# Two channels at once on even and odd rows in the first transform stage of a long-convolution and maxout kernel

## The chip, the core and the metric

The kernel runs on one core of a Trainium2 chip. A core has five engines with queues of their own: TensorE (PE; its weight loads are listed as PEld), VectorE (DVE), ScalarE (ACT), GpSimd (POOL) and SyncE (SP, which issues DMAs). Matmul results land in PSUM; everything else works in SBUF. PE, DVE and ACT reach PSUM, POOL does not. The metric is the device time of one execution in microseconds. Before the change it is 2269.31 us, the median of three runs (2269.03 to 2272.66).

## What is computed

```python
# x, v: (4, 12544, 128); the filter is the same for all four batches
h_filt = (np.maximum(pos_emb @ w1, 0) @ w2) * np.exp(-0.01 * pos)[:, None]
u = x * v
y = irfft(rfft(u, n=2*S, axis=1) * rfft(h_filt, n=2*S, axis=0), n=2*S, axis=1)[:, :S]
t = (x * y).reshape(4 * 12544, 128)
h = np.maximum(np.maximum(t @ moe_w1, t @ moe_w2), t @ moe_w3)     # 768 wide
out = h @ moe_w_out
```

A causal convolution of 12544 positions for each of 128 channels and four batches, then a maxout layer with three input matrices and one output matrix. All of it is in float32. The weights of the maxout arrive as float64 words and are converted on the chip; two of the three input matrices are kept as differences from the first (max(a, b, c) = a + max(max(b-a, 0), c-a)), and the first one is folded with the output matrix into `lin`.

## The kernel before

**The convolution in stages.** A sequence of 12544 is laid out as 98 rows (NB) of 128. Its transform of length 128 x 90 (N1 = 90) is done in two stages with a fixed small table each. The first stage works over the 98 rows, for each channel. The second one works over the 128 places within a row, and its tables differ for each of 45 pairs of frequencies (NK = 45). Then come the product with the filter's transform and the same two stages backwards.

**A unit** is four channels (`NU` = 32 units a batch). For batches 1 to 3 a unit goes through these steps, each a function that the plan places in a slot:

- `u_load` (SP): two DMAs of 196 KB, x and v with the places within a row reversed, 128 partitions x 4 channels x 98. The tiles come from the pools `inp` (3 buffers) and, for every fourth unit, `inq`.
- `u_mul` (DVE): the product x v, in place.
- `u_planes` (POOL): the low and high 16 bits of each number are copied to two planes of a tile `planes`, padded from 98 to 128 columns with zeros by a memset (lines 395 and 396).
- `u_dma` (SP): one transposing DMA of the planes into `turned`.
- `u_join` (ACT one half, DVE the other): the two halves of each number are put together again, in `uT`: 98 rows by 16 stacks of 64, for two units. Each tile `uT` belongs to two units, of which each writes a half.
- `u_first`, which is `u_products` and what it returns (line 418): the matmuls. For each of four channels, each half h and each part c (real, imaginary), a stack of uT (98 x 64) is the stationary operand and 90 columns of the table `f1q` move: 16 matmuls a unit, output in 64 partitions each, two column blocks. Line 440 copies the part h = 0 out of PSUM (ACT, `high`), and line 445 writes the sum and the difference with the part h = 1 to `spec` (two DVE operations of 360 elements).

Units 0 to 5 of batch 1 take a different way (`u_turn`): PE transposes them during the prologue, four transposes to a bank of PSUM, and ACT copies the bank out.

**The pairs of frequencies.** `spec` holds the result of the first stage for a whole batch: 128 partitions x 90 x 2 x 128 channels. When all 32 units are done, `q_load` takes rows of it for the frequencies of two steps g to a tile `sq`, in four DMAs of 32 partitions (SP, lines 467 to 471). `g_quarter` (PE, lines 496 and 506) does the second stage of step g and the backward one of step g - 3 in 64x64 blocks, `g_fold` (ACT, DVE) sums them, `q_swap`, `q_re`, `q_im` (ACT, DVE, POOL) multiply by the filter, `q_unfold` (two DVE operations, line 552) makes sum and difference, and `g_store` (POOL queue) writes the result to DRAM. I call the time in which units run a unit stage, the rest of a batch its pair stage.

**The maxout beside it.** All this runs beside the maxout of the previous batch, which is cut into 32 tiles of 392 positions and each tile into six slots (NF = 6). A slot is one `up` (four matmuls of 392 columns into two of three banks `hps`, a Relu on ACT at line 771, a max on DVE at line 774) and one `down` (two matmuls into `ops`). Each tile also needs `t_load` (DMAs), `t_sums` (two operations, on POOL while units run, otherwise on DVE), `t_last` (the last backward stage, PE, into a bank of the pairs `cps`) and a store. There are 192 slots a batch, and PE runs them in the order of the program text.

**The plan.** `conv_steps(b, done)` (line 609) gives each step a slot. A unit's place is `s = (u - done) * UNIT * per_pair + lead`; its load comes nine slots earlier, mul six, planes five, dma four, the join at s, the product two later. `UNIT` is 0.6 (line 702), `lead` is 1 for batches 2 and 3 and 6 for batch 1, whose units 0 to 5 are done in the prologue and at the start. The first pair of frequencies starts seven slots after the last unit's place. With these numbers `per_pair` is 2.63 slots for batches 2 and 3 (units every 1.58 slots, product of unit 31 in slot 51, first quarter in slot 56) and 2.71 for batch 1 (1.62, 48 and 53). A negative slot lies in the batch before.

The products of units 0 and 1 of batch 1 are made in the prologue (`unit`, line 1102), those of 2 to 4 by hand in the first slot of the maxout (lines 1195 to 1225).

## Time and profile before

| what | value |
|---|---|
| median of three runs | 2269.31 us |
| span of the profiled execution | 2267.5 us |
| PE busy | 2252.4 us (99%) |
| DVE, ACT, POOL busy | 1563.7, 1176.0, 876.7 us |
| first-stage matmuls, L428 into cps | 2960 instructions |
| ACT copy of the part h = 0, L440 | 93 times, 797 ns |
| DVE sum and difference into spec, L445 | 186 times, 789 ns |
| POOL copy to planes, L396 | 90 times, 847 ns |
| sq from spec | 264 DMAs of 128 KB, 6.4 us to landing |

One execution was recorded. Lines of the page give the engine, the line of the program, the operation, the tile written and the tiles read. Matmuls are pipelined, so the busy time of a group counts overlapping ones together; distances between starts tell their pace. A float32 matmul is listed as two instructions, and each has a weight load. "128*64" in a matmul is its rows (contraction) by its columns (output partitions). The chain that ended last is followed back from the last instruction, at each step to what released it. The rows of windows give, for each engine, the busy time and number of instructions in a stretch, then the granted clock, the mean busy share of the 16 DMA engines and GB/s.

### The profile page before, as it was taken

Reading aid. Unit: us, or ns where it says so; the run is one execution under the profiler, and the core shown is the slowest. Engines: PE = TensorE matmul, PEld = TensorE weight load, DVE = VectorE, ACT = ScalarE, POOL = GpSimd, SP = SyncE. Lnnn points to the kernel's source line nnn. Section 1 sums busy time; section 2 is a strip of 40 time slices with the busy share of each in tenths; the row PEclk is TensorE's granted clock in tenths of the full one; section 3 lists DMA queues with packets and bytes.
Section 4 is the critical chain, followed back from the end, with each engine's and each line's share of the span. In section 5 each row is a group of like instructions: output and inputs, shape, how many; then the busy total and the mean of one; then the engine's idle time right before and its main releaser. Section 6 shows DMA issues by size and latency. Waiting matters only on the chain.

```text
span 2267.5 us, 68405 instructions
## 1 busy us (share of the span) xinstructions
PE 2252.4 (99%) x27855; PEld 1356.9 (60%) x27855; DVE 1563.7 (69%) x2859; ACT 1176.0 (52%) x2131; POOL 876.7 (39%) x1090
## 2 busy tenths in 40 slices
PE   9999999999999999999999999999999999999998
PEld 8999866555555556655555556655555556666665
DVE  5589967678778667668888757667888754454443
ACT  3688844466666534456666534456666522222222
POOL 1145434223333234323333234323333326666666
PEclk9999999999999999999999999999999999999999
DMA  8788999889989599989999699889999732222221
GB/s 194 179 248 277 298 201 183 168 201 233 243 220 248 158 187 185 174 190 239 241 236 238 181 180 185 160 195 239 232 245 232 194 82 56 58 70 67 56 56 23
DMA packets 473324, 411.03 MB, mean 181 GB/s; under 512 B 327997, under 2 KB 374526, under 8 KB 473009
## 3 DMA queue, kind: packets, MB, share of 16 engines
q1 hardware_dynamic: 445929, 329.31, 64.4%
q0 software_dynamic: 26288, 75.62, 10.9%
q8 instruction: 219, 3.59, 0.7%
q10 hardware_dynamic: 792, 1.72, 0.3%
q14 instruction: 96, 0.79, 0.1%
HBM read 262.84 MB, written 84.67 MB: 153 GB/s over the span
## 4 chain that ended last, share of the span: by engine, by line
PE 99%; DMA 0%; issue 0%; ACT 0%; POOL 0%; DVE 0%; POOLq 0%; ACTq 0%; DVEq 0%
PE hps L156 45%; PE ops L156 20%; PE ops L834 6%; PE cps L428 5%; PE ps L156 4%; PE cps L156 4%; PE cps L496 3%; PE ps L165 3%; PE cps L506 3%; PE sps L1066 2%; PE gps L1048 2%; PE last L156 1%; PE ps L380 1%; PE ps L342 1%; DMA wt<-wt_const 0%; DMA zt<-zd 0%
## 5 line engine op out<-in xcount | busy, mean ns | idle before, releaser
L156 PE MATMUL hps<-gt,w_sb 128*64 128x392 f32 x6144 | 1146.2, 494 | 0.1
L771 ACT ACTIVATE hid<-hps 128x392 f32<-128x392 f32 x768 | 384.1, 500 | 699.6 <-PE hps L156 680.6
L156 PEld LDWEIGHTS hps<-gt,w_sb 128*64 128x64 f32 x6144 | 421.2, 137 | 430.8 <-issue 401.3
L774 DVE TENSOR_TENSOR hid<-hid,hps 128x392 f32<-128x392 f32 x768 | 428.0, 557 | 335.6 <-PE hps L156 323.0
L156 PE MATMUL ops<-hid,wo_sb 128*64 128x392 f32 x2304 | 477.1, 492 | 0.0
L548 POOL TENSOR_TENSOR cb<-cb,xs 128x512 f32<-128x512 f32 x135 | 173.9, 1288 | 474.7 <-DVE xs L545 384.1
L156 PEld LDWEIGHTS ops<-hid,wo_sb 128*64 128x64 f32 x2304 | 166.0, 137 | 213.1 <-issue 213.1
L521 DVE TENSOR_TENSOR cb<-cps,eo 128x512 f32<-128x512 f32 (+1 forms) x288 | 175.1, 649 | 76.1 <-ACT eo L518 76.1
L445 DVE TENSOR_TENSOR spec<-cps,high 128x360 f32<-128x360 f32 (+1 forms) x186 | 139.2, 789 | 104.7 <-ACT high L440 104.7
L789 POOL DMA_DIRECT2D out_dram<-ot x96 | 75.6, 788 | 335.2 <-ACT ot L787 282.3
L536 ACT ACTIVATE xs<-cb 32x512 f32<-32x512 f32 x270 | 169.6, 628 | 21.1 <-DVE cb L521 12.1
L537 ACT COPY xs<-cb 32x512 f32<-32x512 f32 x270 | 166.3, 616 | 3.2
L440 ACT COPY high<-cps 128x360 f32<-128x360 f32 x93 | 73.9, 797 | 169.7 <-PE cps L428 144.9
L552 DVE TENSOR_TENSOR xs<-cb 128x256 f32<-128x256 f32 x270 | 144.4, 580 | 7.7 <-POOL cb L548 7.7
L428 PEld LDWEIGHTS cps<-f1q,uT 98*64 98x64 f32 x2960 | 125.4, 137 | 26.2 <-issue 24.3
L428 PE MATMUL cps<-f1q,uT 98*64 98x90 f32 x2960 | 130.9, 241 | 0.0
L396 POOL COPY planes<-ut 128x784 uint16<-128x784 uint16 x90 | 76.3, 847 | 119.8 <-DVE ut L375 114.1
L529 POOL DMA_DIRECT2D zd<-cb x135 | 92.4, 685 | 63.7 <-DVE cb L521 60.7
L156 PEld LDWEIGHTS cps<-f4p,even 90*64 90x64 f32 x1552 | 87.5, 138 | 35.9 <-issue 34.6
L858 POOL DMA_DIRECT2D out_dram<-o x128 | 77.5, 610 | 51.5 <-DVE o L851 49.1
L156 PE MATMUL cps<-f4p,zt 90*64 90x49 f32 x1552 | 95.8, 222 | 0.0
L156 PE MATMUL cps<-f4p,even 90*64 90x49 f32 x1552 | 94.5, 220 | 0.0
(152 smaller groups left out, 3150.5 us busy)
## 6 DMA issues: line engine op xcount, KB each, us to landing
ht<-hd SPq DMA_DIRECT2D x264, 256.0 KB, 6.5
wt<-wq_const SPq DMA_DIRECT2D x144, 256.0 KB, 6.2
zd<-cb POOLq DMA_DIRECT2D x135, 256.0 KB, 5.7
zt<-zd SPq DMA_DIRECT2D x384, 90.0 KB, 3.0
sq<-spec SPq DMA_DIRECT2D x264, 128.0 KB, 6.4
ut<-in_xr_dram SPq DMA_DIRECT2D x128, 196.0 KB, 4.0
ut<-in_vr_dram SPq DMA_DIRECT2D x128, 196.0 KB, 4.4
xT<-in_x_dram SPq DMA_DIRECT2D x256, 98.0 KB, 3.4
```

Source lines behind the costliest of these rows:

```text
L156: nc.tensor.matmul(out[64 * h:64 * h + 64], lhsT[:, 64 * h:64 * h + 64], rhs, start=start, stop=stop, skip_group_check=True)
L428: nc.tensor.matmul(ps[64 * c:64 * c + 64, 256 * i + h * N1:256 * i + (h + 1) * N1], t[:, 2 * ((at + i) % 8) + h].rearrange("n r t -> n (r ...
L445: nc.vector.tensor_tensor(out=spec[:, :, a, at:at + n], in0=v[:, 1], in1=highs[0], op=op)
L521: nc.vector.tensor_tensor(out=cb[:, a, lo:hi], in0=ps[:, lo:hi], in1=eo[:, lo:hi], op=op)
L529: nc.gpsimd.dma_start(zd[b][2 * z:2 * z + 2].rearrange("k c t a f -> (k c t) a f"), zss.pop(z))
L536: nc.scalar.mul(xs[at:at + 32], xt[at + 32:at + 64], -1.0)
L537: nc.scalar.copy(xs[at + 32:at + 64], xt[at:at + 32])
L548: nc.gpsimd.tensor_tensor(out=xts[g], in0=xts[g], in1=xs[:], op=ALU.add)
L552: nc.vector.tensor_tensor(out=ab[:, q], in0=y[:, 0], in1=y[:, 1], op=(ALU.subtract, ALU.add)[q])
L771: nc.scalar.activation(h[:], pa[:, 0:N], Relu)
L774: nc.vector.tensor_tensor(out=h[:], in0=h[:], in1=pb[:, 0:N], op=ALU.max)
L834: nc.tensor.matmul(ps[64 * c:64 * c + 64, 0:H2], w, rhs[:, H2 * c:H2 * c + H2], start=start, stop=True, skip_group_check=True)
```

## The change

The first stage of batches 1 to 3 is split by even and odd rows. The 98 rows become two sets of 49 (HB); the even ones sit in partitions 0 to 48 of `uT`, the odd ones in 64 to 112. `u_planes` sorts the columns in this way (one memset, now two copies of half the size), so that the transposing DMA delivers both sets; `u_turn` does it with eight matmuls against the identity in place of four transposes, and two copies by ACT. The table `f1e` has 49 rows in each half and only every second of the frequencies (45 real, 45 imaginary columns), since the others follow from sums and differences of the two sets.

A call of `u_products(x)` now belongs to two units: of each it takes two channels (d picks the unit's channels, and the 64 output partitions). It is 2 x 2 x 2 x 2 = 16 matmuls of 49 x 64 by 90 columns: the row set p picks partitions 0 to 48 or 64 to 112 and one of two banks, d picks the output partitions. ACT copies the bank of the even set (`high`), DVE writes sum and difference with the bank of the odd set to a new tile `sums` (two operations of 360), and POOL makes the second level of sums from it, into `spec`: two operations of 180 elements and four of 90. Two calls serve two units and stand in the same slot, at odd units, moved by one or two slots where t_last is.

`spec` now has the units' channel halves in the partitions and the real and imaginary parts in the free dimension, so `q_load` issues eight DMAs in place of four, in pieces of 64 numbers. `u_join` has ACT copy both halves. `q_unfold` gives its second operation to POOL. `inq` goes. `UNIT` is 0.8 with a lead of -14 for batches 2 and 3 and 0.7 with a lead of 6 for batch 1: `per_pair` is 2.61 and 2.60 slots, units come every 2.09 and 1.82 slots, the last products are in slots 52 and 53, the first quarters in 57 and 58.

```diff
-    f1q = np.stack([np.concatenate([up.real, up.imag], 1), f1], 1)
+    f1e = np.zeros((64 + NB // 2, 2, N1))
+    for p in range(2):
+        for h, t in enumerate((up, a)):
+            t = t[p::2, ::2]
+            f1e[64 * p:64 * p + NB // 2, h] = np.concatenate([t.real, t.imag], 1)
...
-        return inp if u < EARLY or u % 4 < 3 else inq
+        return inp
 
     def u_load(b, u):
-        c, g0 = divmod(u, NG // 4)
+        c, g0 = divmod(u if b == 0 else u // 2 + u % 2 * (NU // 2), NG // 4)
...
-            uts[u] = uts[u + 1] = utp.tile([NB, 16, 2, 32], FP32, tag="uT", name="uT")
-        ps = state["turn"]()
-        turn(u, ps)
-        nc.scalar.copy(uts[u][:, 8 * (u % 2):8 * (u % 2) + 8],
-                       ps[0:NB, :].rearrange("n (s t r) -> n s r t", s=8, r=2))
+            uts[u] = uts[u + 1] = utp.tile([P, 16, 2, 32], FP32, tag="uT", name="uT")
+        ps, (a, _) = state["turn"](), us.pop(u)
+        for i in range(4):
+            for p in range(2):
+                nc.tensor.matmul(ps[64 * p:64 * p + HB, i * P:(i + 1) * P], a[:, i, p::2], eye[:],
+                                 start=(i == 0), stop=True, skip_group_check=True)
+        for n in (0, 64):
+            nc.scalar.copy(uts[u][n:n + HB, 8 * (u % 2):8 * (u % 2) + 8],
+                           ps[n:n + HB, :].rearrange("n (s t r) -> n s r t", s=8, r=2))
...
-        pl_ = cvp.tile([P, 2, 4, P], U16, tag="cb", name="planes", bufs=3)
-        nc.gpsimd.memset(pl_[:, :, :, NB:], 0)
-        nc.gpsimd.tensor_copy(
-            pl_[:, :, :, 0:NB], a[:].bitcast(U16).rearrange("p s (n h) -> p h s n", h=2))
+        pl_ = cvp.tile([P, 2, 4, P], U16, tag="pl", name="planes", bufs=3)
+        w = pl_[:].rearrange("p h s (e m) -> p h s e m", e=2)
+        nc.gpsimd.memset(pl_[:].rearrange("p h s (e m) -> p (h s e) m", e=2)[:, :, HB:], 0)
+        for h in range(2):
+            nc.gpsimd.tensor_copy(
+                w[:, h, :, :, 0:HB],
+                a[:].bitcast(U16).rearrange("p s (m e h) -> p h s e m", e=2, h=2)[:, h])
...
-            copies[h](
-                uts[u][:, 8 * (u % 2):8 * (u % 2) + 8].rearrange(
+            nc.scalar.copy(
...
-    def u_products(u, i0=0, n=4, ps=None, tag="eo"):
-
-
-        t = uts[u] if i0 + n < 4 else uts.pop(u)
-        held = ps is not None
-        ps = (ps if held else state["bank"]())[:, 0:256 * n]
-        at = 4 * u + i0
-        for i in range(n):
+    def u_products(x, banks=None, tag="eo"):
+
+
+        u, w = x - x % 2, x % 2
+        t = uts[u]
+        held = banks is not None
+        if not held:
+            ps = state["bank"]()
+            banks = ps[:, 0:512], ps[:, 512:1024]
+        for i in range(2):
             for h in range(2):
-                for c in range(2):
-                    nc.tensor.matmul(
-                        ps[64 * c:64 * c + 64, 256 * i + h * N1:256 * i + (h + 1) * N1],
-                        t[:, 2 * ((at + i) % 8) + h].rearrange("n r t -> n (r t)"),
-                        f1q[:, h, c * N1:(c + 1) * N1],
-                        start=(i % 2 == 0 and h == 0), stop=True, skip_group_check=True)
-        v = ps.rearrange("p (s m) -> p s m", m=256)[:, :, 0:2 * N1].rearrange(
-            "p s (h k) -> p h k s", h=2)
-        highs = []
+                for p in range(2):
+                    for d in range(2):
+                        nc.tensor.matmul(
+                            banks[p][64 * d:64 * d + 64, N1 * (2 * i + h):N1 * (2 * i + h + 1)],
+                            t[64 * p:64 * p + HB, 8 * d + 4 * w + 2 * i + h].rearrange(
+                                "n r t -> n (r t)"),
+                            f1e[64 * p:64 * p + HB, h], start=(i == 0 and h == 0), stop=True,
+                            skip_group_check=True)
+        at = 2 * x
+        v = spec[:].rearrange("p (k x) a (c d) -> p x a c k d", x=2, c=2)[..., at:at + 2]
+        made = []
 
         def top():
-            high = cvp.tile([P, n, D], FP32, tag=tag, name="high", bufs=2 if tag == "eo" else 3)
-            highs.append(high[:, :, 0:N1].rearrange("p s k -> p k s"))
-            nc.scalar.copy(highs[0], v[:, 0])
+            high = cvp.tile([P, 4 * N1], FP32, tag=tag, name="high", bufs=3 if tag == "xs" else 2)
+            nc.scalar.copy(high[:], banks[0][:, 0:4 * N1])
+            made.append(high)
 
         def both(ops=(0, 1)):
-            for a in ops:
-                op = (ALU.add, ALU.subtract)[a]
-                nc.vector.tensor_tensor(out=spec[:, :, a, at:at + n], in0=v[:, 1],
-                                        in1=highs[0], op=op)
+            if len(made) < 2:
+                made.append(cvp.tile([P, 2, 4 * N1], FP32, tag=state["wide"][0], name="sums",
+                                      bufs=state["wide"][1]))
+            high, sums = made
+            for k in ops:
+                nc.vector.tensor_tensor(out=sums[:, k], in0=high[:], in1=banks[1][:, 0:4 * N1],
+                                        op=(ALU.add, ALU.subtract)[k])
+                y = sums[:, k].rearrange("p (i h c k) -> p h c k i", i=2, h=2, c=2)
+                for a in range(2):
+                    for c in range(2) if k else (slice(None),):
+                        nc.gpsimd.tensor_tensor(
+                            out=v[:, k, a, c], in0=y[:, 1, c], in1=y[:, 0, 1 - c if k else c],
+                            op=(ALU.add, ALU.subtract)[a ^ (1 - c) if k else a])
...
-                nc.sync.dma_start(
-                    t[64 * r + 32 * c:64 * r + 32 * c + 32, 0:n].rearrange(
-                        "p x k a d -> p (x k a d)"),
-                    spec[64 * c + 32 * r:64 * c + 32 * r + 32, 2 * g:2 * g + 2 * n].rearrange(
-                        "p k a d -> p (k a d)"))
+                for d in range(2):
+                    at, of = 64 * r + 32 * c, 64 * d + 32 * r
+                    nc.sync.dma_start(
+                        t[at:at + 32, 0:n].rearrange(
+                            "p x k a (d f) -> p d (x k a) f", d=2)[:, d],
+                        spec[of:of + 32, 2 * g:2 * g + 2 * n].rearrange(
+                            "p k a (c f) -> p c (k a) f", c=2)[:, c])
...
-        nc.vector.tensor_tensor(out=ab[:, q], in0=y[:, 0], in1=y[:, 1],
-                                op=(ALU.subtract, ALU.add)[q])
+        (nc.vector, nc.gpsimd)[q].tensor_tensor(
+            out=ab[:, q], in0=y[:, 0], in1=y[:, 1], op=(ALU.subtract, ALU.add)[q])
...
-        lead, low = (1, -NT * NF) if b > 1 else (6, 0)
+        lead, low, UNIT = (-14, -NT * NF, 0.8) if b > 1 else (6, 0, 0.7)
...
-            at(int(s + 2), 1, u_first, u)
+            if u % 2:
+                on = int(s + 2)
+                on += (0, 0, 2, 1, 0, 0)[on % NF]
+                at(on, 1, u_first, u - 1)
+                at(on, 1, u_first, u)
...
-        for h in range(2):
-            u_first(u, 2 * h, 2)
+        top, both = u_products(u, (bank(), bank()), "x")
+        top()
+        both()
```

## Prediction

> **What bounds the kernel now.** I read the page first: busy times, then the chain that ended last.
>
> ```profile
> PE 2252.4 (99%) x27855; PEld 1356.9 (60%) x27855; DVE 1563.7 (69%) x2859; ACT 1176.0 (52%) x2131; POOL 876.7 (39%) x1090
> PE 99%; DMA 0%; issue 0%; ACT 0%; POOL 0%; DVE 0%; POOLq 0%; ACTq 0%; DVEq 0%
> ```
>
> PE is the bound from end to end, and its instructions run in program order: whatever shortens its stream shortens the kernel, and whatever makes it wait lengthens it one for one. So I need the pace of the stream, not the busy column (which counts overlapping matmuls together). The timeline of PE gives it as the distance between starts. A unit of the first stage, and a short 64x64 stage in the prologue:
>
> ```profile
> 903.83 1.41 PE L428 MATMUL cps<-f1q,uT 98*64 98x90 f32 x32
> 905.07 1.49 PE L156 MATMUL hps<-gt,w_sb 128*64 128x392 f32 x8
> ...
> 30.43 1.46 PE L165 MATMUL ps<-f1q,uT 98*64 98x90 f32 x32
> 31.82 1.74 PE L342 MATMUL ps<-w_sb,specH 64*41 64x64 f32 x64
> 33.48 1.08 PE L380 MATMUL ps<-eye,ut 128*98 128x128 f32 x8
> ```
>
> One unit takes 905.07 - 903.83 = 1.24 us for 32 instructions (16 fp32 matmuls, two passes each): 38.9 ns apiece. L342, in 64x64 blocks over 64 columns, takes 33.48 - 31.82 = 1.66 us for 64: 26 ns apiece. The quarter stage shows 64x64 blocks over 128 columns, and what it costs to go in and out of them:
>
> ```profile
> 1112.64 0.83 PE L156 MATMUL ops<-hid,wo_sb 128*64 128x392 f32 x4
> 1113.40 0.67 PE L496 MATMUL cps<-sq,wt 64*64 64x128 f32 x16
> 1113.89 0.62 PE L506 MATMUL cps<-xs,wt 64*64 64x128 f32 x16
> 1114.33 0.62 PE L496 MATMUL cps<-sq,wt 64*64 64x128 f32 x16
> 1114.76 0.62 PE L506 MATMUL cps<-xs,wt 64*64 64x128 f32 x16
> 1115.31 1.54 PE L156 MATMUL hps<-gt,w_sb 128*64 128x392 f32 x8
> 1116.68 0.83 PE L156 MATMUL ops<-hid,wo_sb 128*64 128x392 f32 x4
> ```
>
> The third group follows the second after 0.44 us for 16: 27.2 ns apiece. Entry and exit cost more: the "ops" group before it lasts 0.76 us (0.66 elsewhere), the first 0.49, the last 0.55, the "hps" group after it 1.37 (1.32 elsewhere): 0.10 + 0.05 + 0.11 + 0.05 = 0.31 us a visit.
>
> **PE, the gain.** After the change two units together are 32 matmuls, so still 64 instructions, over 90 columns in 64x64 blocks. No row has that shape. L342 (64 columns) says 26 ns, the quarter stage (128 columns) 27.2. If four blocks simply ran twice as fast as today's two, 38.9 / 2 = 19.5 ns. I take 26, since going from 128 columns to 64 hardly moved the pace, which looks like a floor per instruction. Two units: 64 x 0.026 + 0.31 = 1.97 us, against 2.48 now: 0.51 saved, 48 pairs in batches 1 to 3: 24.5 us. By 27.2 ns it is 20.7, by 19.5 it is 44. Back goes the turning of units 0 to 5 of batch 1: four transposes at 0.126 us (the eight after 33.48 take 1.01) become eight two-pass matmuls, 16 instructions at about 0.06 (half of 0.126, one pass of 64 columns' width): 0.5 more for each of six, 3 us. Net 21.5 us, bounds 18 to 41.
>
> **ACT and DVE.** Each unit's second join copy moves from DVE (0.58) to ACT (0.78), and units 0 to 5 get a second 0.6 us eviction. The sums stay two DVE operations of 360, but contiguous. Half of q_unfold (135 x 0.58) leaves DVE. ACT is busy 23 of 50 us in a unit stage and DVE 35, so these lie beside PE and I cost them at nothing; without that cover the 90 join copies would be 70 us.
>
> **POOL, the new work.** The rows nearest in kind, and the share of POOL in a unit stage (850 to 900) and in a pair stage (1100 to 1150):
>
> ```profile
> L548 POOL TENSOR_TENSOR cb<-cb,xs 128x512 f32<-128x512 f32 x135 | 173.9, 1288 | 474.7 <-DVE xs L545 384.1 <-ACT hid L771 67.5 <-ACT eo L518 8.4
> L396 POOL COPY planes<-ut 128x784 uint16<-128x784 uint16 x90 | 76.3, 847 | 119.8 <-DVE ut L375 114.1 <-DMA ut<-in_vr_dram 4.0 <-DMA turned<-planes 1.8
> L804 POOL TENSOR_TENSOR hid<-hid 128x392 f32<-128x392 f32 x48 | 47.4, 1016 | 0.0
> L977 POOL COPY spec<-wo_sb 128x256 f32<-128x256 f32 x3 | 1.7, 596 | 2.5 <-PE ps L165 2.5
> 850.00:900.00 50.00, 50.00 (x654) 30.97 (x652) 35.44 (x62) 22.82 (x40) 22.01 (x32) 1.00 0.94 185
> 1100.00:1150.00 50.00, 50.00 (x592) 26.57 (x594) 40.90 (x71) 31.36 (x57) 15.74 (x17) 1.00 1.00 245
> ```
>
> A call of u_products adds six two-input operations, 720 elements in all (two of 180, four of 90). L548 and L804 (medians 1.27 and 1.02 us) give 2.1 ns an element and 0.2 us a start: 720 x 2.1 + 6 x 0.2 = 2.7 us. But those rows are contiguous, and the new operations read every element 720 bytes from the last and write runs of two. The nearest row with short runs is L977: 0.53 us (median) for 256 in runs of four, where L396's 1.07 ns an element gives 0.27, so about 1 ns an element extra. One such extra makes 3.4 us a call; on both inputs and the output, 4.9. I take 2.9, near the rows of the same operation, and keep 1.5 (no start cost) to 4.9. The planes become a memset (0.30) and two copies, 1.05 together.
>
> Now the room. A tile of the unit stage is six slots of up and down (1.98 each), 0.66 for lin, 0.92 for t_last: 13.5 us, plus units. In batches 2 and 3 units come every 0.8 x 2.61 = 2.09 slots, 2.87 a tile at 0.99 us: 16.3 us of PE. POOL: the two sums of t_sums 2.6, an output issue 0.8, 2.87 x (2.9 + 1.35) = 12.2: 15.6, so 96%. In batch 1 (0.7 x 2.60 = 1.82 slots, 3.3 units a tile) PE needs 16.8 and POOL 3.4 + 14.0 = 17.4: over by 0.6 for 7.6 tiles, 5 us, of which the head start of planes (issued five slots, some 13 us, before the join) hides most. I charge 3 us, bounds 0 to 100. Behind a late sum on POOL stand the planes, behind them the transposing DMA on SP and every load SP has after it, then ACT's join, then PE.
>
> The Trainium skill speaks against this change here: "GPSIMD Engine Reference", section 7, says that a read whose step exceeds 8 bytes costs about 2.9 cycles an element where a near one costs 1.9. No row here shows such a read. By it (an estimate: one cycle at 1.2 GHz more on each of two inputs) a call would take 2.7 + 1.2 = 3.9 us, and the total would land about 30 us above before.
>
> **The loads of sq.** q_load issues eight DMAs instead of four, in 256-byte pieces instead of 4096. On SP, four take 2.42 us of the 13.5 between two quarter pairs; SP's issues fill 159 of 230 us in 1050 to 1280, and four more a pair make 69% into 87%. On the DMA engines, the packet records show 4096-byte packets of this queue at 235 ns in that window and 256-byte ones at 18 (median) to 28 (mean) in 850 to 950: 128 x 235 / 16 = 1.9 us a pair becomes 2048 x 18..28 / 16 = 2.3 to 3.6, where the share is already 0.91 to 1.00. Today the last sq lands 3 to 9 us before its quarter; four more issues eat 2.4 of that. What is late next is the quarter itself. I charge 0.1 us for each of 69 pairs, 7 us; bounds 0 (the slack holds) to 0.6 a pair, 41.
>
> The lead of -14 moves the loads of three units and their transposes into the end of the previous pair stage; u_first itself starts at slot -8, after the last q_load has read spec, so I see no new wait on spec. The pool inq goes, but units come a third less often: nothing, unless POOL is late, which is priced above.
>
> **Sum.** 2267.5 - 21.5 + 3 + 7 = 2256. The profiled span lies 1.8 us under the median of 2269.3, so 2258.
>
> **Rivals.** First, POOL becomes the bound of the unit stages. The strided reads and the 96% speak for it, the unshaken 1.27 us of its contiguous sums against. It decides from about 3.0 us a call; at 3.4, POOL needs 17.0 a tile in batches 2 and 3 (0.7 over, 11 tiles each) and 19.1 in batch 1 (2.3 over): 15 + 17 = 32, less 10 that the head start absorbs: 2267.5 - 21.5 + 22 + 7 + 1.8 = 2277, slower. Second, the sq loads: at 0.6 us a pair, 2269.3 - 21.5 + 3 + 41 = 2292. The DMA share of 1.00 speaks for it, the slack of 3 to 9 us against. Third, no floor at 26 ns: 2269.3 - 41 + 10 = 2238; the quarter stage's 27.2 at full columns speaks for it, L342 against. Fourth, the blocks do not pair by rows and nothing is gained on PE: 2282; the 64x64 rows all but exclude it.
>
> **Chances.** My forecast (2245 to 2264) 0.52, POOL 0.22, sq 0.16, no floor 0.07, no pairing 0.03. What a measurement can tell from no change is 0.2%, 4.5 us: faster than 2264.8 takes my forecast, the third rival and the mild end of the first, 0.57; the same 0.09; slower 0.34. The range is 2238 to 2294: below it some 5%, above it the hard ends of the first two, some 12%.
>
> **What would show it.** Right: L428's successor at 1.6 to 1.8 us for 64 instructions, POOL's six operations summing to under 3.0 us a call, planes copies without a growing distance from the unit's product, quarter starts still 13.5 us apart. Wrong: POOL busy 50 of 50 in a unit stage, "hid" or "high" of ACT waiting on "turned", DVE's sums waiting for POOL, or PE in L496 waiting on "sq<-spec".

## The result, and the profile after

The changed kernel takes 2381.57 us, the median of five runs (2377.82 to 2397.18), beside 2270.2 us of the kernel before on the same chip: a ratio of 1.050 (1.0478 to 1.0522). It is 111 us slower, where 2258 was forecast with a range up to 2294. The profiled execution is the slowest of the five; its span is 2395.3 us, 127.8 us over the span of before.

The page, busy times and chain, as they were shown of the kernel before:

```profile
PE 2272.1 (95%) x27927; PEld 1316.7 (55%) x27927; DVE 1569.8 (66%) x2624; ACT 1215.6 (51%) x2223; POOL 1338.5 (56%) x1893
PE 36%; DMA 8%; SPq 3%; DVE 3%; POOL 2%; issue 1%; ACT 0%; DVEq 0%; POOLq 0%; ACTq 0%
```

The shares of the chain are of the whole span. After the change the chain can be followed back only to 1122 us, so its shares add up to 53%, of which PE has 36: PE is no longer alone in it, as it was with 99% before. The stretches that the prediction used (columns: PE, PEld, DVE, ACT, POOL busy, granted clock, DMA share, GB/s) show where:

```profile
850.00:900.00 50.00, 45.66 (x552) 22.82 (x550) 33.53 (x44) 22.45 (x42) 45.61 (x77) 0.93 0.74 132
1100.00:1150.00 50.00, 50.00 (x552) 25.71 (x546) 36.92 (x64) 32.10 (x58) 21.25 (x24) 1.00 1.02 230
```

In a unit stage PE idles 4.3 of 50 us, at a granted clock of 0.93 where it was 1.00, and POOL is busy 45.6 where it was 22.0, without its DMA issues. To see what each stage lost, I take from the traces the distance between the starts of the same maxout tile's first product with `lin`, tile by tile. Against the kernel before, the start up to the first of these tiles is 5.3 us longer, the unit stages (tiles 0 to 9 of each batch, and 27 to 31 of the batch before, where the next units lead in) 72 us, the pair stages (tiles 10 to 26, and the end of the last batch) 50 us.

**PE's own part did get shorter, more than forecast.** The timeline, start and length of a group:

```profile
920.60 1.48 PE L446 MATMUL cps<-f1e,uT 49*64 49x90 f32 x64
922.01 1.54 PE L164 MATMUL hps<-gt,w_sb 128*64 128x392 f32 x8
```

Two units take 922.01 - 920.60 = 1.41 us, 22 ns an instruction, where they took 2.48. A group of 32 of the same instructions (at 285.00 us) takes 0.78, so the second 32 cost 0.63, 19.7 ns apiece, and the way in and out costs some 0.15. As the forecast said of such blocks, the neighbours grow too: the four-instruction group before takes 0.75 us in place of 0.66, the eight-instruction one behind 1.37 in place of 1.32. That leaves 2.48 - 1.41 - 0.15 = 0.92 us a pair of units, 44 us over 48 pairs. So the losses are not 127.8 but about 172 us, most of them in the unit stages.

108 of the 172 are waits: PE idles 2395.3 - 2272.1 = 123 us of the span, before 15. Some 38 more are a slower clock: its mean over the span is 0.980, before 0.999, and by the trace's record of it PE does 77 us of its work at half clock. 16 of the 20 stretches at half clock begin during a wait of PE of 1.6 us or more, or within 1.5 us after it. What remains, some 26 us, isn't placed.

**POOL's new work, by groups** (busy, mean ns of one, then idle before):

```profile
L472 POOL TENSOR_TENSOR spec<-sums 128x90 f32<-128x90 f32 x384 | 187.9, 522 | 0.0
L472 POOL TENSOR_TENSOR spec<-sums 128x180 f32<-128x180 f32 x192 | 154.2, 825 | 57.2 <-DVE sums L467 56.9
L410 POOL COPY planes<-ut 128x392 uint16<-128x392 uint16 x180 | 97.5, 577 | 31.1 <-DVE ut L383 31.1
...
L383 DVE TENSOR_TENSOR ut<-ut 128x392 f32<-128x392 f32 x128 | 209.2, 1635 | 38.5 <-DMA ut<-in_vr_dram 36.0 <-PE ps L388 1.3 <-PE ps L173 0.7
```

The last one in the kernel before:

```profile
L375 DVE TENSOR_TENSOR ut<-ut 128x392 f32<-128x392 f32 x128 | 75.9, 595 | 20.3 <-DMA ut<-in_vr_dram 20.2
```

A call costs 2 x 0.825 + 4 x 0.522 = 3.74 us. The surprise is u_mul on DVE, which nothing changed: its mean is 1635 ns in place of 595. One of the places, in the timeline:

```profile
901.10 6.65 POOL L472 TENSOR_TENSOR spec<-sums 128x180 f32<-128x180 f32 x12
901.13 8.27 DVE L383 TENSOR_TENSOR ut<-ut 128x392 f32<-128x392 f32 x1
907.72 1.25 POOL L774 TENSOR_TENSOR even<-zt 90x512 f32<-90x512 f32 x1
909.05 1.48 POOL L774 TENSOR_TENSOR zt<-zt 90x512 f32<-90x512 f32 x1
909.32 1.02 DVE L808 TENSOR_TENSOR hid<-hid,hps 128x392 f32<-128x392 f32 x2
909.92 2.88 PE L164 MATMUL hps<-gt,w_sb 128*64 128x392 f32 x8 [6.47 <-DVE hid L808]
```

u_mul begins as POOL's twelve sums do and ends 8.27 us later, after POOL has got through them and the first of t_sums without a pause. It ends soon after the 0.08 us between the two sums of L774. The max of the maxout stands behind it on DVE, and PE waits 6.47 us for that max. The wait costs more than its length: the eight matmuls behind it take 2.88 us where such a group takes 1.54 (at 922.01 above), and the granted clock is recorded at half there, from 905.8 to 916.0 us. Of the 96 u_muls of batches 1 to 3, 35 last over 1 us; the 96 together are 138 us over 0.555 us each. Not every u_mul that meets POOL's sums is held like this one: of the 44 that begin while a sum runs, 24 are through in less than 1 us, and 15 take 3 to 8.3 us. What decides between them was not found.

PE's longest waits over the whole span (total us, times, longest):

```profile
PE hps L164 <- DVE hid L808: 54.4, 19, 8.2
PE cps L526 <- DMA sq<-spec: 16.7, 23, 2.1
PE cps L164 <- POOL zt L774: 9.6, 10, 1.0
```

The first is the wait for the max behind DVE. The second is the sign of the pair stages: PE, in the quarter's product L526, now waits for `sq`; before it never did. The third and a smaller one of the same kind, 12.0 us together, are for the sums of t_sums on POOL (L774), which come late to t_last; two more, 7.2 us, are for those that DVE makes, so that t_sums costs 19.2 us in all. The units' product L446 waited 0.3 us in all, and never for its input `uT`.

### The profile page after: what moved, and what is told of

It is laid out like the page before. It is cut to its first block, busy times and chain, and to the rows that moved or that the text cites. A ratio compares the mean times of both kernels' runs of the same rounds, so it can differ in the third digit from the quotient of the medians.

```text
span 2395.3 us, 69820 instructions
## 1 busy us (share of the span) xinstructions
PE 2272.1 (95%) x27927; PEld 1316.7 (55%) x27927; DVE 1569.8 (66%) x2624; ACT 1215.6 (51%) x2223; POOL 1338.5 (56%) x1893
## 4 chain that ended last, share of the span: by engine, by line
PE 36%; DMA 8%; SPq 3%; DVE 3%; POOL 2%; issue 1%; ACT 0%; DVEq 0%; POOLq 0%; ACTq 0%
PE hps L164 20%; PE ops L868 5%; PE ops L164 5%; DMA sq<-spec 3%; DMA ht<-hd 2%; DMA wt<-wq_const 1%; POOL spec L472 1%; PE cps L164 1%; DMA zt<-zd 1%; PE last L164 1%; DMA xT<-in_x_dram 1%; PE cps L536 1%; PE cps L526 1%; SPq L497 1%; DVE hid L808 1%
## 5 line engine op out<-in xcount | busy, mean ns | idle before, releaser
L164 PE MATMUL hps<-gt,w_sb 128*64 128x392 f32 x6144 | 1170.5, 503 | 55.9 <-DVE hid L808 54.4
L808 DVE TENSOR_TENSOR hid<-hid,hps 128x392 f32<-128x392 f32 x768 | 427.1, 557 | 422.4 <-PE hps L164 405.9
L164 PE MATMUL ops<-hid,wo_sb 128*64 128x392 f32 x2304 | 485.2, 500 | 0.0
L472 POOL TENSOR_TENSOR spec<-sums 128x90 f32<-128x90 f32 (+1 forms) x576 | 335.9, 623 | 57.2 <-DVE sums L467 56.9
L383 DVE TENSOR_TENSOR ut<-ut 128x392 f32<-128x392 f32 x128 | 209.2, 1635 | 38.5 <-DMA ut<-in_vr_dram 36.0
L426 ACT COPY uT<-turned 113x512 uint16<-113x512 uint16 x180 | 125.9, 770 | 4.3 <-DMA turned<-planes 4.2
L526 PE MATMUL cps<-sq,wt 64*64 64x128 f32 x2160 | 96.7, 280 | 25.0 <-DMA sq<-spec 16.7
L467 DVE TENSOR_TENSOR sums<-high,cps 128x360 f32<-128x360 f32 x186 | 85.9, 522 | 49.2 <-ACT high L458 49.2
L582 DVE TENSOR_TENSOR xs<-cb 128x256 f32<-128x256 f32 x135 | 94.3, 712 | 34.2 <-POOL cb L578 34.2
L410 POOL COPY planes<-ut 128x392 uint16<-128x392 uint16 x180 | 97.5, 577 | 31.1 <-DVE ut L383 31.1
L582 POOL TENSOR_TENSOR xs<-cb 128x256 f32<-128x256 f32 x135 | 113.8, 861 | 1.1
```

Of the source, the lines that this page charges most:

```text
L164: nc.tensor.matmul(out[64 * h:64 * h + 64], lhsT[:, 64 * h:64 * h + 64], rhs, start=start, stop=stop, skip_group_check=True)
L383: nc.vector.tensor_tensor(out=a[:], in0=a[:], in1=v[:], op=ALU.mult)
L426: nc.scalar.copy(uts[u][0:HR, 8 * (u % 2):8 * (u % 2) + 8].rearrange("n s r t -> n (s r t)").bitcast(U16).rearrange("n (s r t h) -> n h s ...
L472: nc.gpsimd.tensor_tensor(out=v[:, k, a, c], in0=y[:, 1, c], in1=y[:, 0, 1 - c if k else c], op=(ALU.add, ALU.subtract)[a ^ (1 - c) if k e ...
L526: nc.tensor.matmul(ps[64 * a:64 * a + 64, at:at + D], w[64 * r:64 * r + 64, k, a, :], t[64 * r:64 * r + 64, k, a, :], start=(k == 0), stop ...
L582: (nc.vector, nc.gpsimd)[q].tensor_tensor(out=ab[:, q], in0=y[:, 0], in1=y[:, 1], op=(ALU.subtract, ALU.add)[q])
```

## The experiments

All are medians of the device time; the kernel before ran beside each of them at 2270.1 to 2271.5 us. Stage columns are us of the profiled span against the kernel before, taken as above. What follows the last of the counted tiles stands in no column; it is 2.6 to 3.4 us longer in split_pool and in the runs from all3 on, all3_act aside, and within 0.6 us of before in the others.

| run | us | ratio | start | unit stages | pair stages |
|---|---|---|---|---|---|
| the change | 2381.6 | 1.050 (1.0478 to 1.0522) | +5 | +72 | +50 |
| sums_dve | 2357.5 | 1.038 (1.0364 to 1.0399) | +8 | +30 | +48 |
| unfold_dve | 2411.4 | 1.062 (1.0571 to 1.066) | +7 | +77 | +61 |
| sums_split | 2405.0 | 1.059 (1.0573 to 1.0611) | +6 | +77 | +50 |
| before_burst | 2270.5 | 1.000 (0.999 to 1.0009) | 0 | 0 | 0 |
| before_burst2 | 2279.1 | 1.0035 (1.0022 to 1.0048) | 0 | +10 | 0 |
| before_sq8 | 2314.7 | 1.019 (1.0167 to 1.0219) | +2 | +1 | +45 |
| before_sq8big | 2299.8 | 1.012 (1.0097 to 1.0146) | +3 | +2 | +28 |
| before_sq4fine | 2277.5 | 1.0037 (1.002 to 1.0054) | +4 | 0 | +10 |
| sq_pool | 2342.7 | 1.032 (1.0302 to 1.0333) | +7 | +27 | +35 |
| sq_big | 2345.4 | 1.033 (1.0297 to 1.0354) | +7 | +30 | +35 |
| sums_apart | 2320.3 | 1.023 (1.0205 to 1.0247) | +5 | -12 | +54 |
| all3 | 2292.9 | 1.010 (1.0086 to 1.012) | +8 | -13 | +25 |
| all3_unfold | 2287.5 | 1.007 (1.0054 to 1.0089) | +7 | -11 | +23 |
| all3_act | 2403.7 | 1.058 (1.0537 to 1.0618) | +6 | -3 | +130 |
| all3_close | 2329.4 | 1.026 (1.0241 to 1.0282) | +5 | +29 | +23 |
| sq_early | 2270.5 | 1.000 (0.9989 to 1.0008) | +8 | -14 | +5 |
| sq_early_split | 2258.5 | 0.994 (0.9929 to 0.9958) | +8 | -25 | +5 |
| split_pool | 2322.3 | 1.023 (1.021 to 1.0249) | +7 | +37 | +5 |

### Who holds DVE

**sums_dve**: the change with its second-level sums on DVE.

```diff
-                        nc.gpsimd.tensor_tensor(
+                        nc.vector.tensor_tensor(
                             out=v[:, k, a, c], in0=y[:, 1, c], in1=y[:, 0, 1 - c if k else c],
```

> The changed kernel with the second level of sums on DVE instead of POOL, all else as changed. Theory A (POOL's unbroken run of 12 two-input operations, 7.5 us a pair, keeps DVE from starting u_mul, which reads two SBUF tiles: 8.27 us in the trace, with the max behind it and PE idle 7.15 us): u_mul falls back to about 0.6 us, the unit stages lose their 72 us of excess and keep PE's gain; DVE pays some 1.2 us a call. 2381 - 72 - up to 48 + 0 to 50 of DVE bursts, so 2265 to 2330, the pair stages' excess of 49 us unchanged. Theory B (the unit stages lose because POOL is simply too slow for its share, 3.74 us a call): about the same time, but then u_mul would have been long only where POOL's queue was full. Theory C (the loss lies in the wider spacing or in joins on ACT): no change, 2370 to 2385.

2357.5 us, above the 2330 that theory A allowed. The mean of u_mul is back at 0.589 us, the mean granted clock rises from 0.980 to 0.993, and the unit stages lose 30 us in place of 72, though DVE now does all the sums. What is left is seen in the same place of the timeline:

```profile
905.54 0.75 DVE L472 TENSOR_TENSOR spec<-sums 128x90 f32<-128x90 f32 x4
906.20 0.56 DVE L808 TENSOR_TENSOR hid<-hid,hps 128x392 f32<-128x392 f32 x1
906.67 0.56 DVE L383 TENSOR_TENSOR ut<-ut 128x392 f32<-128x392 f32 x1
906.81 0.88 PE L164 MATMUL hps<-gt,w_sb 128*64 128x392 f32 x4 [1.79 <-DVE hid L808]
```

The sixteen sums of two calls run on DVE from 900.91 to 906.20, and the max behind them makes PE wait 1.79 us.

**before_burst and before_burst2**: the kernel before with a POOL load that nobody needs, twelve sums of the change's shapes after every fourth unit, from a weight table to a scratch tile. In the first run each sum overwrites the last one's place, so that some of them start 0.08 us after the one before has ended; in the second each has its own place and they follow without a pause.

```diff
     def u_first(*args):
         u_products(*args)()
+        if len(args) == 1 and args[0] > 5 and args[0] % 4 == 3:
+            burst(args[0] % 8 == 3)
```

> The kernel before, plus 12 POOL additions after every fourth unit (two of 180 and four of 90 elements, twice, from the resident output weights to a scratch tile that nothing reads; alternately with the change's distant reads and with near ones). POOL stays under its capacity: 7.5 us for four units of 1.2 us planes each. Theory A: u_mul and other DVE operations with two SBUF inputs stretch to as much as a burst, PE idles behind the max: 2270 + 20 to 90. Theory B: nothing waits for the scratch tile and POOL keeps up: 2268 to 2275. The near bursts against the distant ones give the price of a distant read: 0.39 against 0.52 us for 90 elements if it costs one cycle an input, equal if it costs nothing.

> The burst of 12 POOL additions on the kernel before once more, now each to a place of its own, so that no addition waits for the last one. The first burst had a gap of 0.08 us between any two, and u_mul started within it. Theory A, sharpened (DVE's two-input operations get in only when POOL leaves a gap): u_mul of up to 7 us where it meets a burst, and 2275 to 2310. If bursts without gaps hold nothing up either: 2268 to 2273, and theory A falls.

2270.5 and 2279.1 us. The same u_mul meets the same burst in both. With the pauses:

```profile
871.05 1.81 DVE L375 TENSOR_TENSOR ut<-ut 128x392 f32<-128x392 f32 x1
871.62 8.24 POOL L465 TENSOR_TENSOR idle<-wo_sb 128x180 f32<-128x180 f32 x12
```

and without:

```profile
871.35 7.68 DVE L375 TENSOR_TENSOR ut<-ut 128x392 f32<-128x392 f32 x1
871.91 6.69 POOL L465 TENSOR_TENSOR idle<-wo_sb 128x180 f32<-128x180 f32 x12
```

With pauses u_mul is through after 1.81 us, while POOL's second sum runs, which takes 1.01 us in place of 0.82; without them it is held to the end of the run, 7.68 us, and that tile of the maxout is 6.8 us longer. So the holding is shown by itself, in a kernel that has nothing else of the change, and it can last over the whole run of POOL's operations. It doesn't always: of the 12 u_muls that overlap one of the 21 bursts without pauses, one more is held, for 2.67 us, and ten are through in less than 0.8 us. That the total is only 9 us comes from there. What these bursts hold more often is DVE's half of u_join, a uint16 copy with a single input in SBUF: its mean is 924 ns where the kernel before has 585, its longest 5.03 us where that has 1.47. The change has this copy on ACT.

The Trainium skill names a cause: "SBUF — State Buffer", section "SBUF: two separate sides", says that DVE and GpSimd share a pair of ports under an exclusive lock, which a DVE operation with both inputs in SBUF needs against a GpSimd operation that reads SBUF, and that whoever comes first has it "for the whole instruction". u_mul has both inputs in SBUF; the max L808 takes one from PSUM and keeps its 557 ns. The runs agree on who blocks whom, and for the u_muls that are through after one sum on how long; but others stay out over 6.7 us of twelve instructions, not one. No run here shows the ports themselves.

**sums_split**: of the six sums of a call the two of 180 elements stay on POOL, the four of 90 go to DVE.

```diff
-                        nc.gpsimd.tensor_tensor(
+                        (nc.gpsimd, nc.vector)[k].tensor_tensor(
```

> The changed kernel with the sums' half on POOL (the two operations of 180) and the half of the differences (four of 90) on DVE. By theory A the runs of POOL are 1.65 us long and wait for DVE in between, u_mul stays under 2.5 us; DVE's burst per pair is 3.6 us instead of 5.1 in the run with all sums on DVE, which cost PE a wait of 1.8 us at the max: 2335 to 2355, against 2357.5 there. By theory B (POOL's load): POOL needs 12.2 us a tile of 16.3, the same. If DVE's length were not what keeps PE waiting, 2355 to 2370.

2405.0 us, the slowest but one, far above every expectation. u_mul is nearly free here, as theory A said (a mean of 0.659 us), and the unit stages lose 77 us all the same. The groups of DVE's sums, here and in sums_dve:

```profile
L472 DVE TENSOR_TENSOR spec<-sums 128x90 f32<-128x90 f32 x384 | 186.0, 543 | 3.3
```

```profile
L472 DVE TENSOR_TENSOR spec<-sums 128x90 f32<-128x90 f32 x384 | 77.7, 265 | 3.3
```

The same operation takes twice as long when POOL works on the other half at the same time, 108 us more in all; these sums too have both inputs in SBUF. Here the holding falls on DVE's own sums in place of u_mul. Sharing these sums between the two engines was worse than giving all of them to either.

**split_pool** asks the same of the best arrangement found (sq_early_split, below): everything as there, only the second-level sums go back to POOL.

```diff
-                        nc.vector.tensor_tensor(
+                        nc.gpsimd.tensor_tensor(
                             out=v[:, k, a, c], in0=y[:, 1, c], in1=y[:, 0, 1 - c if k else c],
```

> Base: the run sq_early_split (2258.5 us), everything else as there. Edit: the second-level sums go back to GpSimd, as the change has them; a call is still cut in two, so POOL gets two sums of 180 elements or four of 90 at a time. Theory (POOL's run of sums holds a DVE operation with two inputs in SBUF until the run ends): u_mul is held for some 2 us where the runs meet it and the sums reach spec later, 2265 to 2300 us. Rival (it was only the length of the burst; in short runs POOL relieves DVE): 2245 to 2258 us.

2322.3 us, 64 more than with DVE, outside of what either side expected. Its stretch of a unit stage:

```profile
850.00:900.00 50.00, 46.59 (x608) 23.16 (x608) 36.87 (x46) 22.17 (x42) 47.09 (x82) 0.97 0.80 154
```

POOL is busy 47.1 of 50 us, and its output stores (0.79 us each, about three in 50 us) nearly fill the rest. And u_mul is held all the same, 117 us over its usual length: with next to no pause on POOL, short runs of sums join up into long ones. How much of the 64 us each of the two takes can't be told from this run.

### The loads of sq

**before_sq8, before_sq8big, before_sq4fine**: the kernel before with its four sq loads per pair cut in eight of 256-byte pieces, in eight of 2 KB pieces, and kept at four with 256-byte pieces (a tile with a gap of two numbers after every 64). The destinations of the loads, in this order:

```diff
-                    t[64 * r + 32 * c:64 * r + 32 * c + 32, 0:n].rearrange(
-                        "p x k a d -> p (x k a d)"),
+                for d in range(2):
...
+                        "p x k a (d f) -> p d (x k a) f", d=2)[:, d],
...
+                for k in range(2):
...
+                            "p x k a d -> p (x k) (a d)")[:, at:at + n],
...
+                        "p x k a d f -> p (x k a d) f")[:, :, 0:64],
```

> The kernel before, with each load of sq as two DMAs in pieces of 64 numbers (256 bytes), as the change has it. Theory E: PE waits on sq in the pair stages, 2270 + 45 = 2315. Theory D: the slack of 3 to 9 us hides it, 2270 to 2278.

> The kernel before, with each load of sq as two DMAs of half the rows each: eight issues a pair as in the change, but pieces of 2 KB. If the 44 us of the run with fine pieces come from SP's issuing (8 x 0.73 us a pair and more), 2300 to 2315; if from the number of packets, 2270 to 2278.

> The kernel before, with the four DMAs of sq kept, but in pieces of 256 bytes (the tile sq is padded after every 64 numbers, so that nothing runs on). If packets cost: 2300 to 2315. If issues cost: 2270 to 2280.

2314.7, 2299.8 and 2277.5 us: 44, 29 and 7 more than before. The number of loads is most of it, the short pieces a smaller part. SP's queue in before_sq8 and in the kernel before, a pair's loads:

```profile
1105.29 8.34 SPq L468 DMA_DIRECT2D sq<-spec  x8
```

```profile
1085.65 3.45 SPq L467 DMA_DIRECT2D sq<-spec  x4
```

Eight loads keep SP 8.34 us where four kept it 3.45 (the medians over all pairs are 7.7 and 3.0), and PE's wait for sq in L497 goes from nothing to 20.0 us. The 44 us are nearly what the pair stages of the change lose (50).

**unfold_dve**: the change with both halves of q_unfold on DVE, to see whether POOL's half was the pair stages' loss.

```diff
-        (nc.vector, nc.gpsimd)[q].tensor_tensor(
+        (nc.vector, nc.vector)[q].tensor_tensor(
```

> The changed kernel with both operations of q_unfold on DVE again. Theory D (the pair stages lose 49 us because q_unfold on POOL comes late or holds DVE's two-input operations back): the pair stages return to the time before, 2381 - 45 = 2336. Theory E (they lose it to the 8 fine-grained loads of sq a pair of steps): 2375 to 2385, PE still waits on sq.

2411.4 us, 30 slower, above both theories: it isn't. DVE is fuller in the pair stages and they lose 61.

**sq_pool and sq_big**, on the kernel of sums_dve: half of the eight loads on POOL's queue; or all eight on SP in 2 KB pieces, with spec laid out so that the pieces are long.

```diff
-                    nc.sync.dma_start(
+                    (nc.sync, nc.gpsimd)[d].dma_start(
...
-        v = spec[:].rearrange("p (k x) a (c d) -> p x a c k d", x=2, c=2)[..., at:at + 2]
+        v = spec[:].rearrange("p g a m -> p (g a m)").rearrange(
+            "p (c k x a d) -> p x a c k d", c=2, x=2, a=2, d=64)[..., at:at + 2]
...
-                        t[at:at + 32, 0:n].rearrange(
-                            "p x k a (d f) -> p d (x k a) f", d=2)[:, d],
+                        t[at:at + 32, d, 0:n].rearrange("p x k a f -> p (x k a f)"),
```

> Base: the changed kernel with its second-level sums on DVE (2357.5 us). Edit: of the eight sq loads of a pair, the four with d = 1 are issued on POOL's queue, the four with d = 0 stay on SP; pieces stay 256 bytes. Theory (what the pair stages lose, some 43 us of span over the three batches, is SP's time to issue eight loads where there were four): most of the loss goes, 2357 - 35 = about 2320 us, 2305 to 2338, and the gain lies in tiles 10 to 26 of each batch. Rival (the 256-byte pieces load the DMA queues, whoever issues them): within 8 us of 2357.

> Same base (2357.5 us). Edit: spec and the sq tile are laid out so that each of the eight sq loads moves pieces of 2 KB instead of 256 bytes; all eight stay on SP. Theory of SP's issues: only what the pieces themselves cost goes, by the two tests on the kernel before (44 us with small pieces, 30 with 2 KB) some 13 us, so 2344 us, 2334 to 2352. Rival (the pieces are the cost): the 43 us of the pair stages go, about 2318 us, under 2328.

2342.7 and 2345.4 us. sq_big came as SP's theory said, sq_pool gained 15 us where 35 were expected. PE's quarter products in sums_dve, then in sq_pool:

```profile
L526 PE MATMUL cps<-sq,wt 64*64 64x128 f32 x2160 | 97.4, 280 | 16.3 <-DMA sq<-spec 12.2 <-DMA wt<-wq_const 3.2 <-issue 0.2
```

```profile
L526 PE MATMUL cps<-sq,wt 64*64 64x128 f32 x2160 | 96.7, 278 | 15.5 <-issue 10.6 <-DMA sq<-spec 4.3 <-DMA wt<-wq_const 0.4
```

The named wait fell from 12.2 to 4.3 us, but L526 idles nearly as long, now under "issue", which means that the profile names no releaser. sq_early, below, shows in a later kernel that such a wait is still one for sq. Relieving SP helps in part; the wait under "issue" fits loads on POOL's queue that come late too.

### Bunching, spacing, and a version of the change that is faster

**sums_apart**, on sums_dve: the two calls of a pair in neighbouring slots.

```diff
-                on += (0, 0, 2, 1, 0, 0)[on % NF]
+                on += (0, -1, 2, 1, 0, 0)[on % NF]
                 at(on, 1, u_first, u - 1)
-                at(on, 1, u_first, u)
+                at(on + (u < NU - 1), 1, u_first, u)
```

> Same base (2357.5 us). Edit: the two calls of a pair of units are put in two neighbouring slots instead of one, so that DVE gets 8 sums in a row instead of 16. Theory (what is left of the unit stages' loss is DVE's burst of 5.1 us, behind which the next max waits and PE idles 1.8 us): the unit stages with their lead-in lose some 10 to 25 us less, 2332 to 2348 us. Rival (the loss there comes from where the units stand and how widely they are spaced, not from the burst): 2352 to 2362 us.

2320.3 us, 37 less, more than expected: the unit stages go from 30 us over the kernel before to 12 under it. **all3** adds both edits of sq to it:

> Same base with the three edits together: pieces of 2 KB, half of the sq loads on POOL's queue, the calls of a pair in neighbouring slots. If the two theories hold, the pair stages come back to their old time and the unit stages nearly so: 2357 - 40 - 17 = about 2300 us, 2275 to 2318. If something else holds either loss, over 2318 us. A time under 2270 us would mean that the gain on PE, some 48 us by the 1.0 us saved a pair, comes through as well.

2292.9 us, within its bounds. Then three single edits to all3: q_unfold on DVE alone (all3_unfold), the half of the loads on ACT's queue in place of POOL's (all3_act), and the units as close as in the kernel before (all3_close: UNIT 0.6, lead 1 and 6).

```diff
-        (nc.vector, nc.gpsimd)[q].tensor_tensor(
+        (nc.vector, nc.vector)[q].tensor_tensor(
...
-                    (nc.sync, nc.gpsimd)[d].dma_start(
+                    (nc.sync, nc.scalar)[d].dma_start(
...
-        lead, low, UNIT = (-14, -NT * NF, 0.8) if b > 1 else (6, 0, 0.7)
+        lead, low, UNIT = (1, -NT * NF, 0.6) if b > 1 else (6, 0, 0.6)
...
+                on = min(on, int(share * per_pair + lead) + 2)
```

> Base: the kernel of the run all3 (2292.9 us). Edit: both halves of q_unfold on DVE, as the kernel before had them. Theory (what is left of the pair stages' loss, some 8 us in each, is PE's second half of a quarter, L537, waiting for a half that POOL makes late, behind its products and its sq issues): the pair stages lose 4 to 8 us less each, 2270 to 2282 us. Rival (it is the sq loads, still eight a pair, that come late, and DVE gets fuller): 2290 to 2315 us.

> Same base (2292.9 us). Edit: the four sq loads with d = 1 on ACT's queue instead of POOL's. Theory of POOL's lateness: POOL is free of 2.0 us of issues a pair, ACT gets them; the pair stages gain 2 to 5 us each where ACT has room, 2278 to 2290 us. Rival (ACT, which hands PE its relu tiles, is held by the issues and their waits): 2295 to 2320 us.

> Same base (2292.9 us). Edit: the units stand as close as in the kernel before (lead 1 and 6, 0.6 of a pair's slots each), the last pair's sums held ahead of the first sq load. Theory (the wider spacing gives DVE and POOL room for a pair's sums): the unit stages lose 5 to 20 us, 2298 to 2313 us. Rival (the spacing only moves work from one tile to another): 2288 to 2297 us.

2287.5, 2403.7 and 2329.4 us. The first lies between its two theories: the wait of PE for POOL's half, 3.6 us in all3, is gone, but the quarter's first product is as late as ever. On ACT the loads are worst of all, 111 us more: they stand behind ACT's relus there, and sq makes PE wait 30.3 us; whether it is only that wasn't tried. The wider spacing, with the earlier lead, is a part of the change that helps: without it the unit stages lose 41 us more, twice the most that was expected.

**sq_early and sq_early_split**, on all3_unfold: the loads three slots earlier; then each call's sums cut in two, k = 0 in its slot and k = 1 in the next.

```diff
-                at(s - 4, 0, q_load, g, min(2, NK - g))
+                at(s - (7 if g else 4), 0, q_load, g, min(2, NK - g))
...
-                at(on, 1, u_first, u - 1)
-                at(on + (u < NU - 1), 1, u_first, u)
+                for i, v in enumerate((u - 1, u)):
+                    if u < NU - 1:
+                        at(on + i, 1, u_begin, v)
+                        at(on + i + 1, 0, u_end, v)
+                    else:
+                        at(on, 1, u_first, v)
```

> Base: the run all3_unfold (2287.5 us), in which L527, the quarter's products with sq, still takes some 5 us longer in the pair stage of a batch than before and nothing else there does. Edit: from the second pair on, the sq loads are put three slots earlier, seven ahead of their quarter instead of four; their number, pieces and queues stay. Theory (the loads are late because eight take longer to issue and land than four): the pair stages lose 4 to 7 us less each, 2268 to 2280 us. Rival (SP and the DMA queues have no time left there, so that earlier loads push others back): 2284 to 2300 us.

> As sq_early, and each call's sums are cut in two: k = 0 in its slot, k = 1 in the next, so that DVE gets four sums in a row instead of eight. Theory (PE's stalls of some 9 us in the unit stage of a batch, under ops<-hid and hps, are waits for a max behind DVE's sums): 5 to 8 us less in each batch than sq_early, together 2250 to 2266 us, under the kernel before. Rival (the stall is that of the two PSUM banks, which are now held longer): as sq_early or up to 20 us slower.

2270.5 and 2258.5 us, both as their theories said. The quarter's product in all3_unfold and in sq_early, where only the time of the loads differs:

```profile
L527 PE MATMUL cps<-sq,wt 64*64 64x128 f32 x2160 | 94.3, 277 | 10.6 <-issue 10.6
```

```profile
L527 PE MATMUL cps<-sq,wt 64*64 64x128 f32 x2160 | 85.7, 276 | 0.0
```

The wait is gone and the busy time is the 85.7 us of the kernel before. sq_early_split is faster than it, by 0.57% (0.42 to 0.71). The busy times of its page, and the stretch of a unit stage:

```profile
PE 2227.3 (99%) x27927; PEld 1298.6 (58%) x27927; DVE 1629.3 (72%) x3335; ACT 1216.8 (54%) x2223; POOL 1044.1 (46%) x1458
```

```profile
850.00:900.00 50.00, 50.00 (x622) 25.06 (x620) 39.13 (x97) 27.06 (x51) 22.62 (x37) 1.00 0.94 179
```

PE is the bound again and fills the unit stage, at full clock. The price of the spreading is on PE: each call now goes in and out of its blocks by itself, 0.79 us (863.58 to 864.37) and 0.15 at its neighbours, so that a pair of units saves 2.48 - 2 x 0.94 = 0.6 us in place of 0.92, some 29 us in all. The unit stages show 25 of them; the start takes 8, the pair stages 5, the end 2.6.

## Why the prediction was wrong

- **PE, the gain: right in kind, half in size.** The forecast took 26 ns an instruction as a floor, from a 64-column row and a 128-column row that hardly differed, and saved 0.51 us a pair. There is no such floor for this shape: 19.7 ns and a visit of 0.30 us save 0.92 a pair, 44 us. That is the third rival's term, 19.5 ns and 44 us, and the 0.31 us for a visit held.
- **POOL, the new work: this term was mis-sized, and the first rival was right on the size.** 2.9 us a call were taken, 3.74 measured. By the forecast's own working a tile of batches 2 and 3 then needs 3.4 + 2.87 x (3.74 + 1.45) = 18.3 us of POOL, where PE, with its larger gain, needs 13.5 + 2.87 x 0.78 = 15.7; the tiles 0 to 9 beside batch 2 take 18.9. The rival was to decide from 3.0 us a call. Its price, 2277, was far too low: it was made for 3.4 us, for PE's need before the real gain, and it let the head start absorb 10 us. Its path (late planes, transposing DMA, join, product) isn't where PE stood: L446 never waited for `uT`, while the max behind DVE cost 54.4 us and the late t_sums 19.2. "Unshaken contiguous sums" was no argument for the choice: in before_burst sums of 180 and 90 elements near each other take 0.57 and 0.38 us, of distant ones 0.83 and 0.50, by their single records. Near sums make 2.7 us a call, as the forecast's first sum had it; the distant reads are the 1.0 that was missing. The rule quoted from the skill, 3.9 us, was nearer than my choice among rows. The "about 30 us above before" beside it doesn't follow, though: the rival's own sum at 3.9 us a call gives about 2322, some 50 above.
- **ACT and DVE at nothing: this step failed.** DVE had the room that was counted (it is busy 33.5 of 50 us), but the step asked how long DVE works and not who can hold it. No case of the prediction has POOL stopping DVE: u_mul alone took 138 us more than its usual length, the largest wait of PE is for the max behind DVE, and work at half clock, mostly behind such waits, took another 38 us that no term held. How the loss of the unit stages divides between a POOL that is nearly full and a DVE that POOL holds, the runs don't tell: moving the sums takes both away (sums_dve), and split_pool has both. That sixteen sums in one slot stand ahead of a max wasn't priced either; on DVE alone that was 37 us (sums_apart).
- **The turning of units 0 to 5** was charged 3 us. By the timelines it is about 2: four turnings take 0.87 us in place of 0.57, two 0.97 in place of 0.48. The start is 5 to 8 us longer in every run of the change; in the change itself, PE waits 3.4 us there for a sum of L774, where it waited 0.3 before.
- **The loads of sq: mis-sized.** 0.1 us a pair were charged, 44 us over 69 pairs are 0.64 (before_sq8), just over the upper bound. The slack of 3 to 9 us was read as cover for 2.4 us of extra issues. But the 2.42 us for four loads were the shortest among the pairs, whose median is 3.0, and eight keep SP 4.9 us longer; other loads wait behind them.
- **The units spaced wider** were charged nothing. They save 36 us in all3 against all3_close.
- **The range** took each rival alone and never two together. POOL over by 18.3 - 15.7 = 2.6 us in 22 tiles, and the 44 us of sq, with PE's 44 saved and 3 for the turning, give 2269.3 - 44 + 3 + 57 + 44 = 2329 before batch 1 is counted, over the upper bound without any holding.

## What to carry to other kernels

Before work is moved to GpSimd because it has idle time, look for operations of VectorE that work between tiles in SBUF (here a product of two tiles, and a copy): a run of GpSimd operations without a pause can hold them to its end, here up to 8 us and more, and whatever stands behind them on VectorE too. Sharing one set of sums between the two engines (sums_split) only moved the holding. Count a long wait of TensorE above its length: behind the 6.47 us wait the next matmuls ran at half pace. Twice as many DMAs of half the size are to be charged with their issue time and with what is queued behind them, and if they come late it may be enough to issue them earlier. A stage that is cut into fewer, larger calls hands its consumers larger bursts; spreading the calls over slots was worth 37 and 12 us here, about as much as the saving on TensorE.

## What was not expected of the hardware

- A run of GpSimd operations can keep VectorE's two-input operation out for as long as it lasts (10.1 us at most in the changed kernel); a pause of 0.08 us between two of them let it in. Others get in after one sum: 24 of the 44 that began during one took less than 1 us. VectorE's uint16 copy, with one input, is held too (5.03 us at most in before_burst2).
- In 64x64 blocks with 49 rows, 90-column matmuls get done at one in 22 ns (64 of them in 1.41 us). "TensorE: Matmul & The Clock Gate" in the Trainium skill (Part 1) says that the distance from start to start never falls below about 25 ns. That holds for matmuls that follow one another; here four blocks work side by side, and in the trace starts in different blocks are 5 to 9 ns apart, a round of four every 77 ns.
- A wait for a DMA issued on POOL's queue stands in the profile as "issue", with no releaser named: 10.6 us under L527, which earlier loads took away whole.
